# Gate product on VectorE, spectral weights in natural column order, half products, an adding step that sets even and odd columns apart, and a new instruction order

## Chip, cores, metric

One NeuronCore of a Trainium2 chip runs the whole kernel in one launch. The metric is the device time in microseconds, the median of several runs. The engines are TensorE (PE, with weight loads shown apart as PEld), VectorE (DVE), ScalarE (ACT), GpSimd (POOL) and SyncE (SP, which here only issues transfers); ACT issues a few transfers too.

## The reference

x is 2048 x 512 in bf16. Every row gets a gate g; the output mixes a spectral filter of x with a two-layer network of x.

```python
g = _sigmoid((x * gate_w).sum(-1, keepdims=True))
a = irfft2(rfft2(x) * (w_r + 1j * w_i))          # over rows and columns, w is 2048 x 257
b = (mish(x @ w1 + b1)) @ w2                     # w1 512 x 1792, w2 1792 x 512
return g * a + (1 - g) * b
```

## The kernel before, in words

Everything is written as small named tasks (`G.add`), each with its engine, what it reads and what it writes. The string `ORDER` lists all tasks by name; `_Graph.place` walks it and appends each task to the list of its engine, so the order on each of the five engines is fixed by hand. A name may carry an engine (`:dve`) and the slots of its buffers (`::3` is PSUM bank 3, for b2 buffers two banks from there on; DVE scratch `tmp` has three slots). `_Graph.emit` writes the lists out with semaphore waits for the dependencies and for the last users of a slot. Engines run their lists in order, so a task that waits holds up everything behind it on its engine. SP's list holds most transfers, in order too.

The tasks by stage (t is one of 16 row tiles, q one of 4 frequency groups, h a half of its columns):

- `x0`, `x2`, `x4`, `x8`, `x12` (L529) load x into rA (the number is the first tile); `xt8` to `xt15` (L545) load transposed tiles; `tr0` to `tr7` (L567) transpose the other eight on PE, `evx` moves them to xT in rX.
- `bf` (L580): sum and difference of the two halves of x's columns, on DVE or POOL. `p` (L593): a 128-point transform over rows on PE, `ep` its evacuation from PSUM. `d` (L608): the transform over columns, `ed` its evacuation. `t0` to `t3` (L706): 64 small matmuls each that join the 16 row tiles; `et` evacuates to Y in rC.
- W: the spectral weights come in ten pieces (L544) to rS, and 16 copies `wrm...`, `wim...` (L640 and L641, the second kind reading backwards) put them into rW and rA; `wrn` (L655, a transfer) and `win` (L651, DVE) make the second half of the partitions; `wrc`, `wic`, `wrz`, `wiz` patch one column. In rW and rA a row has 132 columns, the even ones first and the odd ones behind them.
- Filter, for each q and h: two copies `sw` (L724) swap the real and imaginary halves of the partitions of Y into `tmp`, `p1` (L733) multiplies Y by rW, `p2` (L736) multiplies `tmp` by rA, `ad` (L739) adds. `c0`, `e1`, `es`, `xp`, `ead`, `e2`, `e3` treat the edge column (`e3`, L781, writes it back).
- `it` (L794), `eit`, `id` (L834), `ec` (L842) and `ey` (L845): the inverse transforms, down to yb in rA. They begin when the filter of their columns is done and need `inv`, `rft`, `zr`, constants and gate values that are loaded late.
- The network: `m{c}_{f}` (L860) is one block of the first layer, four matmuls of 512 columns, for row chunk c (four tiles) and one of 14 blocks f of w1; `h{c}_{f}` (L865) is mish on ACT. 56 such groups. `n{t}` (L878) is the second layer for one tile, 14 matmuls; `ip` (L886, L904) adds the spectral part on PE, `o` and `fin` (L892, L895, L908) scale by the gate, `out` stores. Chunk 3's h is stored in rS, over the staged W, so the first `h3` waits for all W copies.
- The gate: `gate0` and `gate8` (L676), 32 matmuls of one column each with xT; then in two halves a clamp `zcl` (L685), a power on POOL `ez` (L687), `ezb` (L688), `ez1` (L689), `omg` (L690), `gc`. `zt` (L809) transposes it on PE, `zte` (L811) and `zw` send it to DRAM, from where `zr` spreads it.

The first matmuls of the order before, with x0 first, and the place of the last W copies:

```python
x0 tab warm::0 ones ident x2 x4 bf0_1:dve tr0::1 bf2_0:pool tr2::2 evx2:dve cRF x8 graw tr3::3 braw w1_0 evx0:act bf4_0:pool evx3:act bf2_1:dve tr1::4
...
m2_1::3 wim110:dve wic0:pool wrn1 wim101:dve h3_2 ezb8 zt::4 win1 et20:act zte h1_8 sw00_0:dve ez18 sw01_0:dve h3_1 wrz0:dve m0_11::2 h0_11 t3::64
```

Of the kernel before, what the change touches and what calls it, by code (L numbers as in the profile page):

```python
# [333 lines left out]
x0 tab warm::0 ones ident x2 x4 bf0_1:dve tr0::1 bf2_0:pool tr2::2 evx2:dve cRF x8 graw tr3::3 braw w1_0 evx0:act bf4_0:pool evx3:act bf2_1:dve tr1::4  # L334
p2::6 p3 tr7::5 evx1:act w1_4 x12 tr5::0 bf12_0:pool bf4_1:dve bf0_0:dve ep2:act p0::1 p1 ep0:act evx7:dve tr_b::3 evx5:act xt10 tr4::4 tr6::5 p6::6
p7 evx6:act w1_8 bf8_1:dve bf8_0:dve p10::1 p11 xt9 ev_b xt8 m0_0::3 h0_0 cFD wi0s1:sp evx4:dve p4::4 m0_3::0 h0_3 wr0s2:act xt15 ep6:dve ep10:dve
m0_7::6 p5 ep4:act gate0::7 m0_6::3 m1_7::1 wr0s0:sp h0_7 bf12_1:dve h1_7 ebase zcl0 ez0 p8::4 m0_1::2 h0_1 wr0s1:act wr1s0:act wrm001:pool p9 p12::6
p13 ep8:dve p14::0 wr1s1:act ldM0 p15 ep14:dve m1_6::2 m1_2::4 m0_9::5 ezb0 wrm101:pool ep12:act d2::0 d3 ed2:dve d4::6 h0_6 h1_6 h1_2 xt14 d12::2 d5
d13 ed12:dve h0_9 m1_0::4 h1_0 d0::0 d1 ed4:dve wrm011:dve m0_13::5 d8::2 wrm110:pool d9 ed0:act m0_4::4 ed8:act h0_4 wi0s2:act m0_2::0 xt11 h0_2
wi0s0:act wim011:pool h0_13 wim000:pool d6::6 m1_5::1 d7 ed6:dve m0_10::2 d10::3 m0_12::0 xt13 h1_5 m0_5::5 h0_5 xt12 wrm111:pool ldM1 d14::6 h0_12  # L340
d15 ed14:dve m1_9::1 h1_9 h0_10 m0_8::5 h0_8 wi1s1:act m1_3::0 h1_3 wi1s0:sp wim111:pool wim100:pool d11 ed10:act wrm010:dve t0::61 et00:act ez10
wrm000:dve m1_13::5 m1_12::0 h1_12 m2_13::3 h2_13 et01:dve c00 m2_8::4 gate8::1 wim010:dve zcl8 ez8 h1_13 wim001:dve ldM2 win0 wrn0 sw01_1:dve:0
wrc0:pool ldM3 t1::62 et11:act et10:act m1_1::0 h1_1 h2_8 m2_11::5 sw00_1:dve:1 h2_11 m3_1::1 m3_2::2 wrm100:dve t2::63 et21:act c01 m3_5::0 m1_8::5
m2_1::3 wim110:dve wic0:pool wrn1 wim101:dve h3_2 ezb8 zt::4 win1 et20:act zte h1_8 sw00_0:dve ez18 sw01_0:dve h3_1 wrz0:dve m0_11::2 h0_11 t3::64
et31:act m2_4::1 m2_9::2 p1_01:dve p1_00:dve sw11_0:dve:2 wiz0:pool p2_00:pool ad_00:pool sw11_1:dve m2_5::4 m3_10::5 p1_11:dve h2_9 h2_5 m3_3::2
m2_2::4 p2_01:dve p2_11:dve wic1:pool ad_01:pool wiz1:pool ad_11:dve et30:dve c03 h2_4 m2_3::1 h2_3 m2_12::6 sw21_1:dve:2 ldG1 h2_12 h2_2 wrc1:pool
h2_1 c02 zw m1_11::7 m3_13::1 sw31_0:dve:1 wrz1:pool sw31_1:act h1_11 sw21_0:dve sw30_1:dve:0 m2_6::6 h2_6 h3_13 p2_21:dve h3_5 p1_21:dve inv
p1_31:dve m3_12::4 sw30_0:dve h3_3 ad_21:dve p2_31:dve w2_8 ad_31:dve sw10_1:act:2 w2_0 m3_6::3 h3_6 m1_10::7 p2_30:dve edge m2_7::6 omg8 ldG3 h2_7
m3_11::1 h3_11 m3_8::0 h3_8 m2_10::2 h2_10 sw10_0:dve m2_0::3 m3_0::6 p2_10:dve m1_4::1 sw20_0:dve:1 sw20_1:dve p1_20:dve p2_20:dve ad_20:dve m3_4::0
m3_7::2 h1_4 h1_10 p1_10:dve ad_10:dve e1::1 h3_10 es0::1 w2_2 n1_0::7 p1_30:dve ad_30:dve es1 xp1::2 xp2 ead::0 e2::5 h3_7 e3_2 e3_3 h3_4 h2_0  # L350
m3_9::1 h3_0 h3_9 e3_1 it2_0::2 it2_1 e3_0 omg0 o1_0:act it3_0::5 h3_12 ldG0 eit2:dve it3_1 eit3:dve n7_0::0 o7_0:act ldG2 it5_0::2 it5_1 eit5:act
it7_0::6 it7_1 eit7:act it1_0::4 it1_1 n15_0::1 it6_0::2 eit1:dve it4_0::6 it0_0::4 it0_1 eit0:act it6_1 eit6:dve it4_1 n6_0::0 eit4:dve id0::4 id1
id8::2 id9 o6_0:dve id14::6 ec0:dve:1 ey0_1 ey0_0 id15 zr ec8:act:2 n3_0::0 ey8_0 ec14:act:0 ey8_1 ey14_1 n14_0::4 ey14_0 rft rfs ip14_0 o3_0:act
ip15_0 o15_0:act n2_0::5 o14_0:dve id10::2 id4::6 id5 id11 out15_0 ec10:dve:1 ey10_0 o2_0:act ec4:dve:2 ey4_1 id2::0 id3 ey4_0 n0_0::4 o0_0:act
ec2:dve:0 ey2_0 ey10_1 n11_0::5 ip11_0 o11_0:dve id12::6 id13 ec12:dve:2 ey12_1 id6::3 id7 ec6:act:1 ey6_1 ey6_0 n10_0::2 ey12_0 n9_0::5 gc0 ip6::3
fin6 n5_0::4 o5_0:act ip5::6 ip10_0 ip7::7 ey2_1 fin5 ip0::3 out14 ip1::0 n13_0::1 ip13_0 fin1 fin7 ip3::4 out7 n4_0::6 o10_0:dve out11 ip2::0 ip4::7
n12_0::2 fin0 out1 fin2 o4_0:act fin4 ip12_0 out5 o12_0:dve n8_0::3 fin3 out3 ip8_0 o8_0:dve o13_0:act ip9_0 n15_256::6 out13 ip15_256 o9_0:act out9
o15_256:act out15_256
# [3 lines left out]
def _build(nc, A_x, A_w_r, A_w_i, B_x, B_w1, B_b1, B_w2, gate_w, out, merge=8, xtp=8, NWARM=13):  # L362
# [10 lines left out]
    with es:  # L373
# [19 lines left out]
        gw_sb = sb("gw_sb", [128, 4], BF)  # L393
        zcl = sb("zcl", [128, NT], F32)
        junk = sb("junk", [128, 1], F32)
        ebase = sb("ebase", [128, NT], F32)
        ez = zcl
# [11 lines left out]
        Yq = rC[:].rearrange("p (a g h n) -> p a h g n", a=4, g=4, h=2)  # L409
        In = rE[:].rearrange("p (g a k) -> p g a k", g=16, a=4)  # L410
        cinv = rE[:, 0:512].rearrange("p (c m) -> p c m", c=4)
        RFs = rE[:, 2048:4096].rearrange("p (t m) -> p t m", t=NT)
# [9 lines left out]
        EDG = rD[:, 7168:8192].rearrange("p (s c m) -> p s c m", s=2, c=4)  # L422
        cst = w2_sb[:, 0, :]
        RF = w2_sb[:, 1, 0:128]
        FD = cst.rearrange("p (c m) -> p c m", c=4)
        brw = w2_sb[0:18, 1, 128:256]
        ezt = w2_sb[0:NT, 1, 256:384]
        RFT = rE[:, 512:640]
# [537 lines left out]
```

## Time and profile before

| what | value |
|---|---|
| median of three runs | 146.49 us (146.43 to 147.15) |
| the profiled execution, as timed | 148.3 us |
| its span in the profile | 146.3 us |
| mean granted clock of TensorE | 0.965 |
| bytes moved | 17.32 MB, 14463 packets |
| DMA busy, 40 slices | 3999999995364018199910000000010000013132 |

The span is one execution from its first to its last instruction. A slice is 3.66 us; each digit is the busy share in tenths. In a group line, the first number behind the bar is the sum of busy time, the next the mean duration of one in ns, and behind the second bar stands the idle time ahead of such instructions. A duration runs from start to end of one instruction; instructions of DVE that follow each other start a little earlier than the one ahead ends, so the time that one costs in a row of equal ones, called the spacing here, is some 0.07 us less.

### The profile page before, as it was taken

The numbers are of one execution on the slowest core, as the hardware profiler recorded it, in microseconds if no ns is written. First come the engines' busy times: TensorE is split into PE (matmuls) and PEld (weight loads), VectorE is DVE, ScalarE is ACT, GpSimd is POOL, SyncE is SP. The second block draws the span as 40 slices with busy tenths as digits, with TensorE's granted clock in tenths as the row PEclk, the third lists the DMA queues.
The fourth block names the chain that finished last, engine by engine and source line by source line (L and its number), as shares of the span: only waits on it lengthen the run. The fifth ranks groups of instructions, "written<-read, shape, count | busy, mean of one in ns | idle before, by whom it ended". The sixth has DMA issues, their size and how long they took to land.

```text
span 146.3 us, 2775 instructions
## 1 busy us (share of the span) xinstructions
PE 129.9 (89%) x1158; PEld 72.2 (49%) x1174; DVE 97.2 (66%) x131; ACT 65.9 (45%) x97; POOL 40.7 (28%) x30
## 2 busy tenths in 40 slices
PE   7539999999999904996999999999999999999992
PEld 4328665655664501542444465955455454444451
DVE  0397625944999999999999945479418590390440
ACT  4435657785959306551898874612230110101111
POOL 1371540563799963398400000000000000000000
PEclk9995999999999995599999999999999999999999
DMA  3999999995364018199910000000010000013132
GB/s 118 288 349 218 291 192 256 182 291 167 76 139 157 0 39 226 50 283 357 402 64 0 4 0 0 0 4 0 0 54 4 0 0 0 4 73 142 72 143 90
DMA packets 14463, 17.32 MB, mean 118 GB/s; under 512 B 5428, under 2 KB 11444, under 8 KB 14260
## 3 DMA queue, kind: packets, MB, share of 16 engines
q1 hardware_dynamic: 12288, 15.60, 37.5%
q10 hardware_dynamic: 2164, 1.56, 5.7%
q8 instruction: 9, 0.15, 0.4%
q14 instruction: 2, 0.02, 0.0%
HBM read 12.92 MB, written 2.10 MB: 103 GB/s over the span
## 4 chain that ended last, share of the span: by engine, by line
PE 74%; DVE 15%; DMA 4%; issue 4%; ACT 1%; SPq 1%; DVEq 0%
PE ps L878 33%; PE ps L860 26%; DMA rA<-in_A_x_dram 4%; PE ps L593 3%; DVE rA L640 3%; PE ps L834 3%; PE ps L794 2%; PE ps L608 2%; DVE rB L580 2%; DVE rA L641 2%; DVE tmp L724 2%; DVE rW L640 2%; DVE rC L498 2%; DVE gcol L689 1%; PE ps L706 1%
## 5 line engine op out<-in xcount | busy, mean ns | idle before, releaser
L860 PE MATMUL ps<-rX,w_sb 128*128 128x512 bf16 x215 | 51.0, 386 | 2.7 <-DVE rC L498 1.3
L860 PEld LDWEIGHTS ps<-rX,w_sb 128*128 128x128 bf16 x224 | 21.2, 100 | 25.5 <-DVE rC L498 1.8
L878 PE MATMUL ps<-w_sb,hs 128*128 128x512 bf16 x108 | 24.8, 379 | 0.4 <-DVE tmp L842 0.2
L892 ACT ACTIVATE rX<-ps,omg 128x512 bf16<-128x512 f32 (+1 forms) x11 | 7.0, 647 | 36.1 <-PE ps L878 26.6
L865 ACT ACTIVATE hs<-ps,b1f 128x512 bf16<-128x512 f32 x28 | 18.1, 686 | 8.1 <-PE ps L860 6.2
L878 PEld LDWEIGHTS ps<-w_sb,hs 128*128 128x128 bf16 x112 | 10.7, 98 | 12.1
L501 ACT ACTIVATE rC<-ps 128x1024 bf16<-128x1024 f32 x10 | 10.5, 1056 | 8.6 <-PE ps L593 3.8
L878 PE MATMUL ps<-w_sb,rS 128*128 128x512 bf16 (+1 forms) x69 | 12.9, 336 | 0.1
L865 ACT ACTIVATE rS<-ps,b1f 128x512 bf16<-128x512 f32 x14 | 9.2, 691 | 7.5 <-DVE rA L640 6.5
L878 PE MATMUL ps<-w_sb,rD 128*128 128x512 bf16 x54 | 12.3, 379 | 0.2 <-issue 0.2
L908 DVE SCALAR_TENSOR_TENSOR rX<-ps,gcol,rX 128x512 bf16<-128x512 f32 x8 | 5.7, 746 | 9.5 <-PE ps L904 7.0
L865 ACT ACTIVATE rD<-ps,b1f 128x512 bf16<-128x512 f32 x14 | 9.2, 689 | 5.6 <-PE ps L860 5.6
L845 DVE TENSOR_TENSOR rA<-tmp,ps 128x512 bf16<-128x512 f32 x16 | 10.1, 683 | 0.2
L580 DVE TENSOR_TENSOR rB<-rA 128x1024 bf16<-128x1024 bf16 (+1 forms) x7 | 6.6, 967 | 5.4 <-DMA rA<-in_A_x_dram 5.4
L895 DVE TENSOR_SCALAR rX<-ps,omg 128x512 bf16<-128x512 f32 x6 | 4.5, 750 | 8.5 <-PE ps L886 7.6
L498 DVE CAST rC<-ps 128x1024 bf16<-128x1024 f32 x6 | 7.1, 1218 | 3.7 <-PE ps L593 3.7
L498 DVE CAST rE<-ps 128x1024 bf16<-128x1024 f32 x5 | 5.9, 1221 | 5.5 <-PE ps L608 5.5
L878 PEld LDWEIGHTS ps<-w_sb,rS 128*128 128x128 bf16 x70 | 6.8, 98 | 5.5
L498 DVE CAST rF<-ps 128x1024 bf16<-128x1024 f32 x5 | 5.9, 1221 | 4.7 <-PE ps L794 4.7
L878 PEld LDWEIGHTS ps<-w_sb,rD 128*128 128x128 bf16 x56 | 5.4, 98 | 6.5
L593 PE MATMUL ps<-w_sb,rB 128*128 128x128 bf16 x64 | 5.8, 249 | 3.1 <-DVE rB L580 2.4
L736 DVE TENSOR_TENSOR tmp<-tmp,rA 128x1024 bf16<-128x1024 bf16 x7 | 8.4, 1216 | 0.1
(84 smaller groups left out, 163.2 us busy)
## 6 DMA issues: line engine op xcount, KB each, us to landing
w_sb<-in_B_w_dram SPq DMA_DIRECT2D x3, 768.0 KB, 8.4
rF<-c_m SPq DMA_DIRECT2D x4, 512.0 KB, 7.3
rB<-c_g SPq DMA_DIRECT2D x4, 512.0 KB, 7.7
out_dram<-rX SPq DMA_DIRECT2D x7, 256.0 KB, 2.1
rA<-in_A_x_dram SPq DMA_DIRECT2D x3, 512.0 KB, 7.5
rW<-rW SPq DMA_DIRECT2D x2, 528.0 KB, 4.3
w_sb<-in_B_w_dram SPq DMA_DIRECT2D x2, 512.0 KB, 9.2
rS<-in_A_w_r_dram ACTq DMA_DIRECT2D x2, 257.0 KB, 7.3
```

The source lines that it names most:

```text
L498: return e.tensor_copy(out=o(), in_=i())
L501: return e.activation(o(), i(), AF.Copy)
L580: return e.tensor_tensor(out=xu[:, a:b_, uv, :], in0=x_sb[:, a:b_, 0:256], in1=x_sb[:, a:b_, 256:512], op=ALU.add if uv == 0 else ALU.subt ...
L593: ins = e.matmul(bank(b, i)[:, 128 * c:128 * (c + 1)], xu[:, t, uv, e_:256:2], RF, start=True, stop=True)
L640: return e.tensor_copy(out=o_, in_=i_)
L736: return e.tensor_tensor(out=z3(z), in0=z3(z), in1=wi3, op=ALU.mult)
L845: return e.tensor_tensor(out=yb[:, t:t + 2, 256 * h:256 * h + 256].rearrange("p t (i e) -> p t i e", e=2), in0=t4(z), in1=o4(bank(b, 1)), ...
L860: ins = e.matmul(bank(b), w1_sb[:, dt_, 128 * ft:128 * (ft + 1)], xT[:, c, dt_, :, :], start=(dt_ == 0), stop=(dt_ == 3))
L865: G.add(f"h{c}_{ft}", [("act", act(512, 1), lambda e, c=c, ft=ft, b=b: e.activation(hs[c][:, ft, :], bank(b), AF.Mish, bias=b1f[:, ft:ft + ...
L878: ins = e.matmul(bank(b)[:, 0:hi - lo], hs[c][:, ft, 128 * tl:128 * (tl + 1)], w2_sb[:, ft, lo:hi], start=(ft == 0), stop=(ft == NFT - 1 a ...
L892: return e.activation(bs[:, t, lo:hi], bank(b)[:, 0:hi - lo], AF.Copy, scale=omg[:, t:t + 1])
L908: return e.scalar_tensor_tensor(out=bs[:, t, :], in0=bank(b), scalar=gcol[:, t:t + 1], in1=bs[:, t, :], op0=ALU.mult, op1=ALU.add)
```

## The change

- The gate's dot product moves from PE to DVE: `gwm` spreads gate_w over the partitions with one matmul, `gwe` puts it into `tmp`, and 16 tasks `gt` multiply a tile of x by it and sum over the row. The gate's small steps are done once for all 16 tiles.
- rW and rA keep W's columns in natural order (130 to a row). The copies read neighbouring columns; 13 are on DVE, 3 on ACT, none on POOL. Both second halves are made by DVE or ACT (`wrn0`), none by a transfer. W comes in eight pieces.
- The two swaps and the product `p2` of a filter step become two half products `hp`, each on 64 partitions, that read one half of the partitions and write the other. All of the filter is on DVE. `ad` writes to rE instead of in place, and sets even and odd columns apart there; the evacuations `ed` and `et` have another column order. The edge's two copies are gone, `xp2` is in two halves, `e3` one copy instead of four.
- Constants move to other places; `rft`, `inv` and `zr` now lie in rC and wait for the whole filter. w1 comes in four pieces, w2's loads no longer wait for the constants.
- `ORDER` is new: x4 is loaded first; five tiles of the second layer (n7, n6, n4, n5, n0) stand ahead of `it` instead of one (n1).

```diff
+XTP = 8
+W1P = ((0, 2), (2, 6), (6, 10), (10, 14))
+XP = ((0, 2), (2, 4), (4, 8), (8, 12), (12, 16))
-WP = 132
+WP = 130
...
+ebase tab warm::0 x4 ones ident tr6::1 x2 bf4_1:dve bf2_1:pool bf2_0:pool x0 tr4::2 bf4_0:dve w1_2 bf0_0:pool tr5::3 tr2::4 x8 x12 w1_6 cRF evx4:dve
+evx6:dve p4::6 p5 xt11 evx5:dve w1_0 graw::0 braw evx2:act tr3::5 evx3:dve tr_b::0 ev_b ep4:act tr7::2 evx7:dve tr1::1 tr0::3 evx0:dve p6::4 p7 gwm::0
+ep6:dve evx1:act p2::6 p3 w1_10 m0_5::2 gwe:act ep2:act xt8 xt9 bf0_1:pool h0_5 ldM3 m0_4::3 h0_4 gt2 gt5 m1_4::1 h1_4 p0::4 p1 ep0:act m0_3::0 h0_3
+bf8_0:dve bf8_1:dve p8::6 p9 ep8:act xt10 ldM2 bf12_1:dve ldM0 p10::2 p11 ep10:act cFD bf12_0:dve gt14 p12::4 p13 ep12:act m0_6::1 p14::6 m1_6::0 h0_6
+p15 wrs3:act gt1 gt7 m0_8::2 ep14:dve h1_6 gt8 h0_8 ldM1 m0_0::3 h0_0 d2::4 d3 d14::6 wrs0:act d6::0 d7 d15 ed2:act gt13 m0_7::2 h0_7 wrs2:sp ed14:dve
+m0_1::3 h0_1 d0::6 gt11 d1 d8::4 ed0:dve wis2:sp gt12 gt9 d9 ed8:dve ed6:act m1_0::2 h1_0 wis0:sp m2_3::3 d12::6 d13 ed12:dve h2_3 d4::0 d5 ed4:act
+m0_11::2 h0_11 xt15 m2_6::3 h2_6 d10::4 d11 ed10:dve t0::06 et01:act gt10 xt12 gt0 m1_9::2 h1_9 m1_2::3 h1_2 t1::46 et11:dve et00:act wrm111:dve
+et10:act m2_0::2 h2_0 m1_3::3 gt3 t2::06 wrm100:act et21:act wrm110:dve m0_10::4 m2_5::5 wis1:sp wis3:act h2_5 et20:dve c02 m0_2::2 c01 h0_2 gt6 h1_3
+t3::06 gt4 m1_13::5 et31:act et30:act h1_13 gt15 m1_11::2 zcl wim011:act wim101:dve wim110:dve wim100:dve h1_11 m0_12::3 h0_12 m2_9::6 m2_8::7 h2_8
+h2_9 ez m1_1::0 h1_1 m1_10::1 wim111:dve wic1:pool win1:dve wrm101:dve wrc1:pool ezb m2_12::5 xt14 m1_5::2 h1_5 wrs1:sp h1_10 wim000:dve wiz1:dve
+hp31_0::1 m1_7::3 wrm011:act zt::7 h2_12 m2_7::6 h1_7 m2_4::0 h2_4 m2_2::2 hp30_1::2 wrm000:dve h2_2 m0_13::1 wrm010:dve xt13 zte m1_8::7 m3_5::5
+wrm001:dve wim010:dve wrc0:dve h0_10 h1_8 m2_1::3 wim001:dve wrn1:dve wic0:pool win0:dve m3_6::0 hp30_0 h2_1 w2_10 m3_7::2 ldG0 m2_10::4 wrz1:pool
+h2_10 w2_0 ldG2 c03 p1_30 w2_5 m1_12::7 m3_11::3 hp31_1 h1_12 ad_30 h3_11 m3_2::4 h3_2 h0_13 hp21_0::0 wiz0:dve hp10_0::2 hp10_1 m3_12::7 h3_12
+m3_9::3 hp21_1 ez1 omg gc h3_5 h3_9 p1_21 ad_21 hp11_1::0 m3_0::4 wrn0:act n7_0::1 h3_0 zw m3_13::7 m2_13::5 wrz0:dve ldG1 h3_7 m3_10::3 h2_13 n6_0::4
+o6_0:act m3_1::2 c00 n4_0::5 h3_10 p1_31 p1_10 ad_10 h3_1 o7_0:act m3_4::4 hp11_0 h3_13 edge e1::3 m0_9::2 hp01_0::2 p1_11 ad_11 h3_6 hp00_0::0 hp00_1
+hp01_1 n5_0::1 h0_9 o5_0:act p1_00 ad_00 o4_0:act m2_11::7 p1_01 ad_01 ad_31 m3_8::0 xp20::0 xp21 h2_11 xp1::2 ead::1 e2::2 h3_4 hp20_1::0 n0_0::3
+ldG3 h3_8 o0_0:act hp20_0 p1_20 ad_20 e3 rft it7_0::4 it7_1 it6_0::0 eit7:dve it6_1 eit6:act m3_3::7 it0_0::2 it5_0::4 inv it5_1 eit5:dve h3_3 h2_7
+it3_0::0 it3_1 eit3:dve it0_1 eit0:dve n14_0::7 zr it2_0::5 it2_1 it4_0::0 it4_1 eit4:act rfs it1_0::3 it1_1 eit1:act eit2:act n3_0::2 id12::0 id13
...
-        G.add("ev_b", [("dve", 0.25, f_evb)], "small", reads=[bb], writes=["b1f", ("gw", 0)])
...
+        G.add("gwm", [("pe", 0.216, lambda e: e.matmul(bank(gb), one[0:1, :], tb(gwb)[0:1, 512:1024], start=True, stop=True))], "small",
+              reads=[gwb], writes=[gb])
+        evac("gwe", lambda: tb(gwb)[:, 0:512], lambda: bank(gb), 512, [gb], [gwb], "small")
+        t_gt = []
+        for t in range(NT):
+            t_gt.append(G.add(f"gt{t}", [("dve", 0.6, lambda e, t=t: e.scalar_tensor_tensor(
+                out=x_sb[:, t, :], in0=x_sb[:, t, :], scalar=1.0, in1=tb(gwb)[:, 0:512], op0=ALU.mult, op1=ALU.mult, accum_out=zcl[:, t:t + 1]))],
+                "gate", reads=[gwb], writes=[("z", t), ("x", t)]))
...
-            dp = t_bf + t_tr if ri else []
-            base = 64 * ri
+            dp = t_bf + t_tr + t_gt if ri else []
...
-                            i_ = sg[:, 16 * h:16 * h + 16, 0:WP] if pt == 0 else sg[:, 16 * h:16 * h + 16, 256:256 - WP:-1]
-                            i_ = i_.rearrange("p f (k u) -> p f u k", u=2)
-                            o_ = dstv[base + 32 * pt:base + 32 * pt + 32, f0 + 16 * h:f0 + 16 * h + 16, :].rearrange("p f (u k) -> p f u k", u=2)
+                            i_ = sg[:, 16 * h:16 * h + 16, 0:129] if pt == 0 else sg[:, 16 * h:16 * h + 16, 256:127:-1]
+                            o_ = dstv[32 * pt:32 * pt + 32, f0 + 16 * h:f0 + 16 * h + 16, 0:129]
...
-                tg = add("gate", "pe", n * 4 * 0.025, f_gate, [("xT", t) for t in range(t0, t1)] + [("gw", 0)], [gb])
...
-                for j in range(2):
-                    lo = 64 * j
-                    i_ = yv[64 - lo:128 - lo]
-                    G.add(f"sw{q}{h}_{j}", [("dve", 0.37, lambda e, z=z, lo=lo, i_=i_: e.tensor_copy(out=zv(z)[lo:lo + 64], in_=i_)),
...
+                def f_h(e, j, y3=y3, z=z, wi3=wi3, z3=z3):
+                    lo, hi = slice(64 * j, 64 * j + 64), slice(64 - 64 * j, 128 - 64 * j)
+                    return e.tensor_tensor(out=z3(z)[lo], in0=y3[hi], in1=wi3[hi], op=ALU.mult)
...
-                def f_p2(e, z=z, wi3=wi3, z3=z3):
-                    return e.tensor_tensor(out=z3(z), in0=z3(z), in1=wi3, op=ALU.mult)
-
-                def f_ad(e, yv=yv, z=z, zv=zv):
-                    return e.tensor_tensor(out=yv, in0=yv, in1=zv(z), op=ALU.add)
...
+                def f_ad(e, yv=yv, z=z, q=q, h=h):
+                    return e.tensor_tensor(out=Yhq[:, q, h], in0=yv.rearrange("p (x k u) -> p x k u", x=8, u=2), in1=tb(z).rearrange("p (x k u) -> p x k u", x=8, u=2), op=ALU.add)
...
-        dma("inv", rE[:, 0:512], d_inv[:, 1:5, :].rearrange("p c m -> p (c m)"), 0.3, writes=["inv"], deps=t_t)
+        dma("inv", rC[:, 0:512], d_inv[:, 1:5, :].rearrange("p c m -> p (c m)"), 0.3, writes=["inv"], deps=t_fil)
```

Yhq is rE seen as (a, h, x, k, u) with u, the even or odd column, 64 elements apart in memory.

More of the change, by code (lines that the diff above doesn't have):

```diff
@@ L333 @@
 ORDER = """
[L334 to L341, printed above, removed]
@@ L346 @@
[L346 to L349, printed above, removed]
@@ new lines, in _build @@
+        add("zcl", "dve", 0.16, lambda e: e.tensor_scalar(out=zcl[:, :], in0=zcl[:, :], scalar1=80.0, scalar2=-80.0, op0=ALU.min, op1=ALU.max),
+            [("z", t) for t in range(NT)], ["zcl"])
+        add("ez", "pool", 0.9, lambda e: e.tensor_tensor(out=ez[:, :], in0=ebase[:, :], in1=zcl[:, :], op=ALU.pow), ["ebase", "zcl"], ["ez"])
+        add("ezb", "dve", 0.13, lambda e: e.tensor_copy(out=ezb[:, :], in_=ez[:, :]), ["ez"], ["ezb"])
+        add("ez1", "dve", 0.13, lambda e: e.tensor_scalar(out=gcol[:, :], in0=ez[:, :], scalar1=1.0, scalar2=None, op0=ALU.add), ["ez"], ["gcol"])
@@ L779, in _build @@
         G.add("e2", [("pe", 0.2, f_e2)], "edge", reads=[ey_, "edge"], writes=[eb2])
-        for q in range(4):
-            G.add(f"e3_{q}", [("dve", 0.12, lambda e, q=q: e.tensor_copy(out=Y[:, 16 * q:16 * q + 16, 0], in_=bank(eb2)[:, 16 * q:16 * q + 16]))],
-                  "edge", reads=[eb2], writes=[("Yh", q, 0), ("Yh", q, 1)])
+        G.add("e3", [("dve", 0.15, lambda e: e.tensor_copy(out=Yh[:, :, 0].rearrange("p (a j g) -> p a j g", a=4, j=4), in_=bank(eb2)[:, 0:64].rearrange("p (a g j) -> p a j g", a=4, g=4)))], "edge",
+              reads=[eb2], writes=[("Yh", q, h) for q in range(4) for h in range(2)])
         t_it = []
```

195 lines of the change are left out of this document (81 added, 114 removed).

## The prediction, as it was made

> **What bounds the kernel now.** I read the page first (shares of busy time, then the 40 slices), then the list of waits, then the timelines of PE, DVE and POOL.
>
> ```profile
> PE 129.9 (89%) x1158; PEld 72.2 (49%) x1174; DVE 97.2 (66%) x131; ACT 65.9 (45%) x97; POOL 40.7 (28%) x30
> ...
> PE   7539999999999904996999999999999999999992
> ...
> DVE  0397625944999999999999945479418590390440
> ...
> POOL 1371540563799963398400000000000000000000
> PEclk9995999999999995599999999999999999999999
> ```
>
> PE is the bound: nearly full from slice 4 on, with one hole in slices 14 and 15 and a thin head. Beside the hole DVE and POOL are full and PE's clock is halved. The PE timeline shows both places:
>
> ```profile
> 10.52 0.86 PE L593 MATMUL ps<-w_sb,rB 128*128 128x128 bf16 x8 [2.36 <-DVE rB L580]
> ...
> 56.52 0.27 PE L809 MATMUL ps<-identt,ezb 128*16 128x128 bf16 x1 [5.08 <-DVE ezb L688]
> 57.03 1.89 PE L860 MATMUL ps<-rX,w_sb 128*128 128x512 bf16 x4 [0.24 <-ACT rS L865]
> 58.85 1.89 PE L706 MATMUL ps<-rE,rF 32*128 32x128 bf16 x64
> ```
>
> The first number of a line is its start, the second its length, the bracket the idle time ahead of it. After the 5.08 us of idle, four L860 matmuls take 1.89 us (1.03 elsewhere) and 64 of L706 1.89 (1.07): the halved clock costs 1.68 us more. Why DVE was late stands in its waits and rows:
>
> ```profile
> ACT rS L865 <- DVE rA L640: 6.5, 1, 6.5
> ...
> PE ps L860 <- DVE rC L498: 1.3, 1, 1.3
> ```
> ```profile
> L736 DVE TENSOR_TENSOR tmp<-tmp,rA 128x1024 bf16<-128x1024 bf16 x7 | 8.4, 1216 | 0.1
> L733 DVE TENSOR_TENSOR rC<-rC,rW 128x1024 bf16<-128x1024 bf16 x8 | 5.3, 688 | 0.1
> L640 DVE COPY rA<-rS 32x2112 bf16<-32x2112 bf16 x2 | 4.0, 1982 | 0.1
> ```
>
> L736 and L733 have one shape, yet L736 averages 1216 ns against 688: two of seven ran beside a POOL instruction and took 5.00 us together. The rS copies of W end last, ACT's h3 stands behind them, and PE runs out of free banks.
>
> **PE's own work.** Spacings: an mm1 group (four 128x512) 0.8625 us, an mm2 tile (14) 3.02, four 128x128 0.223, a t quarter 1.07. Before, from t0 (37.77) to the inverse transform `it` (86.73): 36 groups 31.05, n1 3.02, four t 4.28, gate 0.78, edge 0.3 = 39.4 in 48.96. The 9.5 lost are 5.08 + 0.24 + 0.33 + 1.30 + 0.48 of small issue gaps + 1.68 of clock, and 0.4 unnamed. The change drops both gate blocks (32 matmuls, 0.78 each) and adds one 128x512 (0.22): PE does 1.34 us less.
>
> **Head.** Before, d began at 24.43 with 9 groups done. x0 and x2 (512 KB) had landed at 5.2, 1 MB at 7.5, 3 MB (x12) at 14.2. In the new order that gives x4 5.2, x2 6.3, x0 7.5, w1_2 9.2, x8 10.8, x12 12.5, w1_6 14.2. DVE sums x4 from 5.2 to 6.5 (0.65 each); POOL does four half-size sums at 1.16 from 6.3 to 10.9, with hardly a DVE sum beside them (in before one DVE sum took 2.34 beside POOL's 2.62). PE waits for x4, then runs transposes, p4 to p7, the gate broadcast and p2, p3 until m0_5 at about 9.5. From there to d2: 8 groups 6.9, eight p 1.8, and p0, p1 0.45 = 9.2, so 18.7. PE idles 1.4 at 3.8 and in pieces afterwards, and in before such a head was followed by a slice at half clock: I add 0.8, d2 at 19.5. d takes 3.57 with 6 groups (5.18) between: t0 at 28.25. This has 14 groups done, before had 20 at 37.77; that is 37.77 - 28.25 - 6 x 0.8625 = 4.3 us earlier, gate included. The x transposes of tiles 8 to 11 are needed at 24.5 now (40 before); xt10 is issued at about 14 by the sum of SP's issue rows (0.5 a plain one, 1.6 to 2.7 a transpose) and takes 7.3 (longest 8.8): landed by 23. W comes in eight pieces instead of ten, with the same bytes, issued from 17 to 24 and landing within 10.2 at the longest row: by 34, wanted from 33 (the first piece, landed by 27) to 48. M0 to M3 are issued ahead of it, by 17, and land in 7.3, where t0 wants them at 28.
>
> **Middle, PE.** 41 groups 35.36, four t 4.28, n7, n6, n4, n5, n0 15.1, edge and zt 0.55, issue gaps 0.64 = 55.9: with no wait, `it` would begin at 84.2.
>
> **Middle, DVE.** Until the clamp of the gate (zcl): it follows t2 (34.9) with an evacuation (1.18), two c0 (0.4) and three gt, so 39.5. The 16 gt are new: 128x512, two inputs with a sum out. Nearest row: L908, the same operation from PSUM, 0.745 long and 0.66 apart; ends: 0.42 (L580 at 512 columns) and 0.82 (0.66 plus a 0.16 small instruction for the sum). I take 0.70: 11.2 us, between the evacuations, where DVE sat idle 1.5 to 2.9 us at a time in before. POOL's power over 16 columns took 1.67 for 8: bounds 1.7 to 3.4, under four W copies either way.
>
> After zcl DVE still has:
> - 11 W copies. Before, they read every second element: 1.24 for 2112 columns. Now they read neighbours, like L724 (0.404 for 1024) and L651 (1.255 for 4224), 0.266 ns a column: 0.68 for 2064. Backwards reads are not shown at this rate; the other end is 1.25, for the four of them 2.3 us more. 7.5.
> - three duplications at 1.25: 3.7. The fourth is on ACT (128x1024 costs 1.02 there: 0.15 + 4160 x 0.85 ns = 3.7), while PE runs n7 and needs no mish; DVE's memset wrz0 waits for it, at about 65 by both counts, and up to 1 us of that stays in the range. They replace two DMA duplications that kept SP's queue waiting until 40.65 and 53.38; now only zw, then edge, hold it, and what stands behind (ldG1, ldG3) is needed at 84.
> - 16 half products at 0.62 (spacing of L733): 9.9, in place of 14 swaps and 7 products. Eight p1: 5.0.
> - eight adds. Six cost 0.62 before; now each output element lands 64 elements from the last one. No row shows that store at this length. Low end: one element a cycle as in L845, 0.61 per 512, so 1.15. For hopping reads: L766 takes 391 ns for 128 columns with W read a row apart, L767 291 without: 0.78 ns each, so 1.15 + 0.75 = 1.9 with rounding. High end: L781 stores 16 hopping elements in 219 ns, L554 14 neighbours in 159: 3.75 ns each, so 5.0; but four of L781 stand only 85 ns apart, so most of that is no rate. I take 1.9, the row with most elements: 15.2.
> - small ones, edge included: 3.2. The evacuations that now set even and odd columns apart read PSUM in hops; L845 does that at 0.61 per 512, so nothing for them.
>
> Sum 44.5, plus three waits for POOL's column copies (0.33 long and two handovers, 0.5 each) 1.5: e3, the last write ahead of `it`, ends at 85.5. That is 1.3 later than PE, so DVE is still the last to arrive, by little.
>
> The Trainium skill ("Vector Engine (DVE) Microarchitecture Reference", 5.2 Measured stream behaviour on trn2) speaks against these adds: a stream that hops at every element takes 1.71 to 1.76 ns a column where neighbours take 1.054, and a store that always steps 24 words takes 2.50. By the first an add would be an estimated 1.83 us and the sum as above; by the second 2.64 and the end near 141. L766 against L767 agrees with the first, for reads and 4-byte elements.
>
> **ACT.** It gains three W copies (1.9 each by its 0.85 ns a column) and loses two swaps; mish needs 0.6 per 0.86 us of PE. I allow 0.5 us for bank waits (0.4 unnamed before). h3 first stands in ACT's order behind the 43rd group, PE near 58, and the last W copy ends near 52: the 5.08 us wait goes, and with it 1.68 of clock.
>
> **End.** Before, `it` to the last matmul (143.51) took 56.78 with 14 tiles and two halves. Four fewer tiles (12.08) and one more group (0.86): 45.6. The constants `inv`, `rft` and `zr` now wait for the last filter; `inv` landed in 2.1 us after issue and is wanted some 10 us after `it` begins, so it hides. The tail stays: 146.3 - 143.5 = 2.8.
>
> **Sum.** 85.5 + 0.5 + 45.6 + 2.8 = 134.4 for the span. The profiled execution of before took 148.3 around a span of 146.3, while the median of the runs is 146.49, 0.2 over that span; so 134.6, and with half a microsecond of doubt towards late, **135.0**.
>
> **The rivals.**
> - *The adds cost one element a cycle (1.15).* DVE ends at 79.5, PE alone decides: 84.2 + 0.5 + 48.4 + 0.2 = 133.3. For: L781's spacing. Chance 0.18, from 131.5 to 133.8.
> - *A store hop costs twice the read hop (2.7 an add), or the backward W copies stay at 1.25 with gt at 0.82.* DVE ends at 92 or 90: 141 or 139. For: nothing in before has such stores at this length. Chance 0.19, from 137 to 143.
> - *The order does less than it says: data come late.* The DMA engines are full until 33 us (the page's DMA row) and much is asked for earlier now: an x transpose or W part that lands 4 us late stops PE or ACT in order, and costs 4 us and up to 1.7 of clock: 138 to 141. Chance 0.09.
> - *Slower: the adds cost what L781's length says (5.0).* Place: the eight adds ahead of e3; PE waits at `it`. 8 x 3.1 = 24.8 more: 159. It decides from 3.5 us an add (12.6 us spread over eight). Against: the 85 ns spacing. Chance 0.09.
>
> **Numbers.** My forecast (134 to 137) has 0.42. Faster by over 0.5% is the forecast and the first three rivals, 0.88; between the third and the last lie 0.03 within 0.5% (0.7 us, about what this measurement can tell); slower 0.09. The range 132 to 142 leaves out the last rival, the far edges of the first and second, about 0.2.
>
> **What would show it.** No PE idle over 1 us between t0 and `it`, clock full there; d from about 19.5 and `it` from 85.5, with e3 just ahead; gt near 0.7, W copies near 0.68 in both directions, adds near 1.9, no DVE row doubled by POOL. Wrong if DVE's adds or gt stand far off, if PE waits for a DMA after 10 us, or if ACT's longer copies leave PE without banks.

## The result, and the profile after

The changed kernel takes **189.19 us** (median of 4 runs, 187.29 to 192.48), the kernel before, timed beside it, 146.82 us (146.43 to 147.45): 1.284 times as long, interval 1.272 to 1.295. The forecast was 135.0 with a range of 132 to 142, so the prediction is wrong, and in its sign. Some executions of a kernel come out over 1.5% longer than its fastest, as 192.48 does here, and the ratios leave these out. The profiled execution took 188.9 us around a span of 186.7.

First the slices of the changed kernel's page (one is 4.67 us here; GB/s is what the DMA engines moved):

```profile
PE   6899799000008999999999800000879999999994
...
PEclk9999999755557999999999975555589999999999
DMA  5999991191199950260000000000011000001413
GB/s 145 364 322 238 377 160 29 33 40 46 49 90 199 379 169 0 52 225 9 0 0 0 0 0 0 0 0 0 4 33 58 0 4 0 32 0 56 183 72 115
```

There are two holes in PE, each five slices wide; the granted clock falls to half in them and stays so for a little behind. Outside of them PE is nearly full from slice 2 on. From slice 6 on and through most of the first hole the DMA engines move 29 to 49 GB/s, against 238 and 377 in slices 3 and 4. The digits of the DMA row do not show how many engines are held: the page counts a packet's whole time in the slice in which it starts, so packets that stand for long leave later slices at one tenth. The list of PE's waits names the holes, and PE's timeline shows their places:

```profile
PE ps L752 <- DVE tmp L745: 24.7, 1, 24.7
PE ps L690 <- issue: 22.9, 1, 22.9
```
```profile
31.98 0.74 PE L690 MATMUL ps<-rE,rF 32*128 32x128 bf16 x40
55.60 0.83 PE L690 MATMUL ps<-rE,rF 32*128 32x128 bf16 x24 [22.88 <-issue]
...
131.12 0.22 PE L752 MATMUL ps<-tmp,rS 128*128 128x1 bf16 x2 [24.67 <-DVE tmp L745]
...
131.68 5.61 PE L854 MATMUL ps<-w_sb,hs 128*128 128x512 bf16 x13 [0.22 <-issue]
...
150.84 2.97 PE L854 MATMUL ps<-w_sb,hs 128*128 128x512 bf16 x13 [0.16 <-DVE tmp L818]
```

The first hole cuts t1 in two after 40 of its 64 matmuls. The matmuls on both sides of it read the same tiles, so no data is missing; "issue" says that the profile shows nothing that PE waited for. The second stands at e2, the edge step, which DVE reaches only at the end of the filter. Behind it 13 matmuls of a tile take 5.61 us, where 13 take 2.97 at full clock.

SP's timeline shows what the transfers did meanwhile. Below it, two groups of DVE show the second hole's cause; the last line is the add of the kernel before (in a group, the number behind the comma is the mean ns of one instruction):

```profile
19.92 30.13 SPq L471 DMA_TRANSPOSE rX<-in_A_x_dram  x2
```
```profile
L715 DVE TENSOR_TENSOR rE<-rC,tmp 128x1024 bf16<-128x1024 bf16 x8 | 37.7, 4754 | 0.2
...
L586 DVE SCALAR_TENSOR_TENSOR rA<-rA,tmp 128x512 bf16<-128x512 bf16 x16 | 11.3, 744 | 0.1
```
```profile
L739 DVE TENSOR_TENSOR rC<-rC,tmp 128x1024 bf16<-128x1024 bf16 x6 | 4.2, 692 | 0.2
```

Two transposes of x took 30.13 us to issue; the sum of SP's rows had put 1.6 to 2.7 on one. L715, the adds, take 4.75 us each where the forecast had 1.9 and the kernel before 0.69 (L739).

The trace's packets tell the rest of the first hole. A merged low piece of W (wrs0, wis0) is 32 packets of 16448 bytes. They went about two at a time: 16.8 us for W_r (23.5 to 40.3), and only then 11.9 us for W_i (40.8 to 52.7). In the kernel before, the 16 packets of the first such piece all started within 0.2 us and took about 1 us each. Something else stood still meanwhile: sixteen packets of 256 and 4 bytes on SP's queue, of the transposes of x by size and place, start near 27 and end together at 53.1, after 25.7 to 26.1 us each and right behind the last of W_i. At 53.1 an instruction packet starts too (the page counts nine of 16 KB each); it landed at 54.2, and PE resumed at 55.6.

### The profile page after: what moved, and what is told of

It is laid out like the page before. It is cut to its first block, busy times and chain, and to the rows that moved or that the text cites. A ratio compares the mean times of both kernels' runs of the same rounds, so it can differ in the third digit from the quotient of the medians.

```text
span 186.7 us, 2660 instructions
## 1 busy us (share of the span) xinstructions
PE 129.2 (69%) x1093; PEld 69.0 (37%) x1111; DVE 123.9 (66%) x158; ACT 76.5 (41%) x101; POOL 10.7 (6%) x16
## 4 chain that ended last, share of the span: by engine, by line
PE 43%; DVE 33%; issue 14%; DMA 5%; ACT 3%; POOL 0%; POOLq 0%; DVEq 0%
DVE rE L715 20%; PE ps L854 18%; PE ps L836 14%; DVE tmp L709 5%; DMA rD<-c_front 3%; DVE rC L712 2%; PE ps L690 2%; DMA rA<-in_A_x_dram 2%; PE ps L810 2%; PE ps L612 2%; PE ps L771 1%; PE ps L862 1%; PE ps L880 1%; PE ps L597 1%; DVE rB L575 1%
## 5 line engine op out<-in xcount | busy, mean ns | idle before, releaser
L715 DVE TENSOR_TENSOR rE<-rC,tmp 128x1024 bf16<-128x1024 bf16 x8 | 37.7, 4754 | 0.2
L868 ACT ACTIVATE rX<-ps,omg 128x512 bf16<-128x512 f32 (+1 forms) x12 | 7.8, 669 | 61.5 <-PE ps L854 37.0
L854 PE MATMUL ps<-w_sb,hs 128*128 128x512 bf16 x107 | 27.4, 409 | 0.6 <-issue 0.4
L502 DVE CAST rC<-ps 128x1024 bf16<-128x1024 f32 x4 | 4.9, 1225 | 26.2 <-PE ps L690 25.2
L505 ACT ACTIVATE rC<-ps 128x1024 bf16<-128x1024 f32 x12 | 12.4, 1069 | 23.9 <-PE ps L690 23.6
L690 PE MATMUL ps<-rE,rF 32*128 32x128 bf16 x256 | 4.8, 223 | 22.9 <-issue 22.9
L752 PE MATMUL ps<-tmp,rS 128*128 128x1 bf16 x2 | 0.2, 177 | 24.7 <-DVE tmp L745 24.7
L690 PEld LDWEIGHTS ps<-rE,rF 32*128 32x128 bf16 x256 | 3.9, 96 | 24.4 <-issue 23.0
L854 PE MATMUL ps<-w_sb,rD 128*128 128x512 bf16 x55 | 12.4, 379 | 0.1
L586 DVE SCALAR_TENSOR_TENSOR rA<-rA,tmp 128x512 bf16<-128x512 bf16 x16 | 11.3, 744 | 0.1
L871 DVE TENSOR_SCALAR rX<-ps,omg 128x512 bf16<-128x512 f32 (+1 forms) x5 | 3.5, 696 | 11.8 <-PE ps L862 7.8
L709 DVE TENSOR_TENSOR tmp<-rC,rA 64x1024 bf16<-64x1024 bf16 x16 | 10.7, 685 | 0.4
L821 DVE TENSOR_TENSOR rA<-tmp,ps 128x512 bf16<-128x512 f32 x16 | 10.2, 681 | 1.0 <-PE ps L810 0.8
```

The lines of the kernel that those rows point to most:

```text
L502: return e.tensor_copy(out=o(), in_=i())
L505: return e.activation(o(), i(), AF.Copy)
L586: t_gt.append(G.add(f"gt{t}", [("dve", 0.6, lambda e, t=t: e.scalar_tensor_tensor(out=x_sb[:, t, :], in0=x_sb[:, t, :], scalar=1.0, in1=tb ...
L690: ins = e.matmul(bank(bp[j // 2], j % 2)[:, 128 * g:128 * g + 128], Mm[r, 4 * q + g, a, :], In[r, 4 * q + g, a, :], start=(a == 0), stop=( ...
L709: return e.tensor_tensor(out=z3(z)[lo], in0=y3[hi], in1=wi3[hi], op=ALU.mult)
L715: return e.tensor_tensor(out=Yhq[:, q, h], in0=yv.rearrange("p (x k u) -> p x k u", x=8, u=2), in1=tb(z).rearrange("p (x k u) -> p x k u", ...
```

## The experiments

Theory: **two faults, each by itself**. (1) The merged W pieces go about two packets at a time, and TensorE's code, which comes as instruction packets among the other DMA packets, is held behind them. (2) The adds' store, which sets each 2-byte element down 64 elements from the last one, costs 4.75 us. The rival to (1): the 22.9 us come from something else in the new order (the transposes, the place in the code). The rival to (2): the adds are dear for their hopping as such, whichever side hops.

**e1_split.** The changed kernel, each merged piece in two:

```diff
...
-            dma(f"{nm}s0", sg[0:64:2], lo, 2.0, queue="sp act", writes=[(nm, "s", 0)])
+            for hh in range(2):
+                dma(f"{nm}s0{hh}", sg[32 * hh:32 * hh + 32:2], lo[hh], 1.0, queue="sp act", writes=[(nm, "s", 0, hh)])
...
```

`ORDER` names the two parts, one behind the other, where it named the piece.

> The changed kernel with each of the two merged W pieces (32 rows of 16448 bytes, one transfer) cut into two transfers of 16 rows, as before the change; nothing else. Theory (serial transfer): the 32 packets of a merged piece went one or two at a time instead of 16 at once, and TensorE's own code, fetched by a transfer as well, stood behind them: the 22.9 us hole inside t1 goes, with some 1.5 us of halved clock; span 160 to 164, packets of 16448 bytes 16 at a time, adds still 4.75 us, TensorE still waiting near 25 us at e2. Rival (the transfers as a whole ask for too much too early, whatever their shape): the hole stays above 15 us, span above 178.

Measured: 168.63 us (168.07 to 170.56), ratio 1.148 (1.139 to 1.157), span 166.5, against 186.7. Its PE waits:

```profile
PE ps L753 <- DVE tmp L746: 24.7, 1, 24.7
PE ps L691 <- issue: 3.1, 1, 3.1
```

The first hole shrinks from 22.9 to 3.1, the second stays. The merge is fault (1); the span lies 2.5 us above the 164 that were expected at most, and the hole that was to go keeps 3.1.

**e2_order.** The changed kernel, with the adds walking in the order of their store, so that the reads hop instead:

```diff
-        Yhq = rE[:].rearrange("p (a h x u k) -> p a h x k u", a=4, h=2, x=8, u=2)
+        Yhq = rE[:].rearrange("p (a h x u k) -> p a h x u k", a=4, h=2, x=8, u=2)
...
-  in0=yv.rearrange("p (x k u) -> p x k u", ...), in1=tb(z).rearrange("p (x k u) -> p x k u", ...)
+  in0=yv.rearrange("p (x k u) -> p x u k", ...), in1=tb(z).rearrange("p (x k u) -> p x u k", ...)
```

> The changed kernel with the eight adds running through the same elements in the order of the store: they write neighbours and read both inputs at a step of two elements; same result in the same place, nothing else. Theory (the hopping store costs): an add falls from 4.75 to 1.15 us, the cost of one element a cycle; the 24.7 us wait at e2 and its halved clock go, span 157 to 161, the 22.9 us hole stays. Rival (the four-dimensional pattern or the two different layouts cost, whichever side hops): adds stay above 3.5 us, span above 178.

Measured: 162.24 us (160.87 to 163.17), ratio 1.101 (1.092 to 1.111), span 161.1. The adds' group and PE's waits:

```profile
L715 DVE TENSOR_TENSOR rE<-rC,tmp 128x1024 bf16<-128x1024 bf16 x8 | 9.7, 1224 | 0.2
```
```profile
PE ps L690 <- issue: 24.7, 1, 24.7
...
PE ps L752 <- DVE tmp L745: 0.3, 1, 0.3
```

The same elements are added, in 1.22 us instead of 4.75: only the side that hops has changed, so the rival to (2) falls. The second hole is gone, the first is whole. In this run the instruction packet that ends the hole is on record from its start: 28.2 us (27.3 to 55.5), where the eight others took 0.9 to 1.4. The packets of the transposes stand here as well, from 27.3 to 54.5.

**e3_both.** Both edits together.

> The changed kernel with both edits: W pieces of 16 rows and adds in the order of the store. If these two are all that the prediction missed, TensorE alone decides and the span is 133 to 136, it begins near 85, no wait of TensorE over 1.5 us after the head. If something else of the new order costs as well, 138 to 146. Slower than before only if neither cause holds.

Measured: 141.65 us (140.3 to 142.36), ratio 0.964 (0.958 to 0.970), so **faster than before**. The spans fall by 20.2 (e1), 25.6 (e2) and 48.5 (both): the faults add up to within 2.7 us. What is left among PE's waits:

```profile
PE ps L691 <- issue: 2.7, 1, 2.7
...
PE ps L772 <- DVE rE L759: 0.7, 1, 0.7
```

The 2.7 are in t1 at the same 40th matmul, and the 64 matmuls of t2 behind them take 1.89 us (1.07 at full clock). So something more than the two faults holds PE there, the second of the two cases that were expected. The packets say that it is code again: counting the later runs too, the trace has eleven holes inside t1 or t3, in nine runs, and at each PE resumes 1.3 to 1.6 us after a 16 KB instruction packet has landed.

**m1_forms.** Single instructions of 128x1024 elements, three of each, and W loads one after the other, with nothing of the computation.

> No part of the computation: single instructions by themselves, each three times and each ended before the next. Adds of 128x1024 in bf16: all neighbours (0.69 expected), the change's hopping store (4.75), the same with neighbours stored and a step of two read (1.15), stores at a step of 2 and of 4 elements, stores in runs of 2, 4 and 16 neighbours, a hopping read on both sides and on one (1.9 by the prediction's price), a hopping store of 4-byte elements, then copies with a hopping store from SBUF and from PSUM, a copy from PSUM with a hopping read (1.22), tensor_scalar and ScalarE's copy with the hopping store. Theory: only stores of lone 2-byte elements are dear (over 4 us), runs of 2 (4 bytes) cost under 2; rival: every hop over 64 bytes costs, whatever its width, so runs of 2 still cost over 2.5 and 4-byte elements over 4. Then transfers one at a time: 32 rows in one transfer to every second partition and to neighbouring partitions, 16 rows in one transfer (twice), 32 rows of 257 in 16 partitions forwards and backwards. Serial theory: both 32-row ones take 15 to 25 us, the 16-row ones 2.5 to 4; rival: all of them take 3 to 6 us when nothing else runs.

Measured, in its groups (L53 stores neighbours; L55 is the changed kernel's add; L57 the same elements in the order of the store; L61 stores every fourth element; L63 and L65 hop between runs of two and of four elements):

```profile
L55 DVE TENSOR_TENSOR o<-a,b 128x1024 bf16<-128x1024 bf16 x3 | 14.1, 4707 | 0.1
...
L61 DVE TENSOR_TENSOR o<-a,b 128x1024 bf16<-128x1024 bf16 x3 | 7.3, 2429 | 0.1
...
L57 DVE TENSOR_TENSOR o<-a,b 128x1024 bf16<-128x1024 bf16 x3 | 3.7, 1226 | 0.1
...
L63 DVE TENSOR_TENSOR o<-a,b 128x1024 bf16<-128x1024 bf16 x3 | 3.1, 1032 | 0.1
L65 DVE TENSOR_TENSOR o<-a,b 128x1024 bf16<-128x1024 bf16 x3 | 2.1, 693 | 0.1
...
L53 DVE TENSOR_TENSOR o<-a,b 128x1024 bf16<-128x1024 bf16 x3 | 2.1, 692 | 0.1
```

The hopping store of lone 2-byte elements costs 4.6 ns an element, runs of two 1.0, runs of four as little as neighbours (0.68). With 4-byte results the same hop takes 1.96 us, on ACT a copy of this form 4.75 (1.06 without hops). The theory holds for this add, but not for every store of lone elements: a step of two costs 1.30 us, a step of four 2.43, a copy from SBUF with the hop of 64 2.49. Hopping reads take 1.23, not the 1.9 of the prediction's price. The merged W load took 18.6 us from its issue to the next, its two 16-row halves 3.7 and 3.5. To neighbouring partitions the merged load took 12.2, below the 15 to 25 that were expected.

**e4_before_merged.** One part of the change alone, in the kernel before: the two low pieces of each W become one.

```diff
...
+ dma(f"{nm}0s0", stg[64 * ri:64 * ri + 64:2], wv[:, 0:64, :].rearrange("q (h l) k -> h q (l k)", h=2), ...)
...
```

> The kernel before with one part alone of the change: the two low W pieces of each array, 16 rows each, become one transfer of 32 rows (W_r on SP's queue, W_i on ACT's), everything else as before. Theory (a 32-row piece of this form is served by one or two DMA engines at a time, about 16 us for its 0.5 MB, and what lies behind it waits, TensorE's code among it): W's copies on POOL and DVE are late or TensorE has a hole with 'issue' before it; 155 to 170 us. Rival (the pieces only hurt in the changed kernel's order, between its transposes of x): within 3 us of the time before.

Measured: 178.93 us (177.71 to 179.65), ratio 1.212 (1.204 to 1.220): the theory's sign, at more than its price. From the waits of all engines:

```profile
POOL rW L644 <- DMA rS<-in_A_w_r_dram: 41.6, 1, 41.6
...
DVE rW L645 <- issue: 33.1, 1, 33.1
...
PE ps L612 <- DVE rE L498: 29.8, 1, 29.8
```

Here it is the data itself that is late. POOL's copy of W waits 41.6 us for the load; DVE stands 33.1 at its own copy from the same staging area (the view names no releaser; that it waits for the load too is argued from its place), with the evacuations of d queued behind, and PE has no bank for 29.8. So this part of the change costs 31 us in the old order too, there by the data and in the changed kernel by the code.

**e5_one_merged.** As e3, but W_r's piece still merged.

> The changed kernel with the adds in store order and W_i's low piece in two transfers, but W_r's low piece still one transfer of 32 rows (on ACT's queue). Theory that each merged piece costs by itself: a hole of 8 us or more inside t1, 147 to 158 us. Rival, that the hole comes from the two in a row (42 to 54 us for the second, behind the first): the hole stays below 4 us and the time is 141 to 144.

Measured: 153.45 us (151.37 to 153.67), ratio 1.035 (1.025 to 1.046).

```profile
PE ps L693 <- issue: 15.5, 1, 15.5
```

One merged piece is enough, and it need not stand on SP's queue with the transposes: this one is on ACT's. It ends at 41.3, though, and the code lands at 46.9. In between W_i's halves, on SP's queue from 26.2 on, go on until 45.3, and packets of the transposes stand until 45.7. In all three runs with a long hole in t1 (the changed kernel, e2, e5) W's pieces, the transposes and the code come free in this order, within 1.6 us. Whether the code stands behind W itself or behind the transposes that W holds up is not shown: no run has a merged piece in this kernel without transposes in flight.

**e6_xt_late** and **e7_xt_late_wic.** What holds the last 2.7 us? e6 is e3 with `xt15` and `xt12` moved behind t3 in `ORDER`; e7 also has `wic1:dve` for `wic1:pool`.

> The kernel with both mended (adds in store order, low W pieces in two transfers), and two of the DMA transposes of x (tokens blocks 15 and 12) issued behind t3 rather than ahead of t0 and t2. Theory (the 2.7 us left inside t1 are TensorE's code held behind traffic that these transposes stretch): the hole falls below 1 us, the granted clock behind it stays above 0.9, 'it' starts 2 to 4 us earlier: 137.5 to 140 us. Rival (the fetch is late at that place of the code whatever the queues hold): the hole stays at 2 to 3 us, 141 to 142.5.

> The last one, and the one-column copy of W_i's second half on VectorE rather than GpSimd, where it waits 3.35 us behind the power of the gate. If VectorE's chain of products sets the start of 'it' once the hole is gone: 1 to 3 us below the last one, 136.5 to 139. If TensorE's own work sets it: the same as the last one within 0.5 us.

Measured: e6 140.74 us, ratio 0.953 (0.946 to 0.960), hole 2.5; e7 139.5 us, 0.944 (0.937 to 0.951), hole 2.6. The transposes were not what holds these last 2.7: the hole kept its size, as e6's rival said. Both times fall between the ranges that were expected for them, and the two intervals overlap, so the 1 us that DVE's wait behind POOL seems to be worth is not settled.

**e8_no_w.** e7 without W's loads.

> The last kernel (both mended, two transposes late, the one-column copy on VectorE) with no spectral weights loaded: their staging area is set to 0.5 by two memsets at the start, so the output is of other weights; all copies and products stay. It takes 2 MB out of the transfers between 18 and 35 us. Theory (the 2.6 us left inside t1 are TensorE's code, asked for near t0's start and held by the traffic): the hole falls below 0.8 us. Rival (two groups of short matmuls one behind the other use up the code faster than it is fetched, whatever the queues hold): the hole stays at 2 to 3 us. The time is then 2 to 3 us lower or the same as the last one within 0.7.

Measured: 135.23 us (135.16 to 135.33), ratio 0.915 (0.910 to 0.920), 4.3 below e7 where 2 to 3 were expected. No hole is left inside a group of matmuls. The windows of e7 and then of e8 (PE, PEld, DVE, ACT and POOL busy, granted clock, DMA share, GB/s):

```profile
30.00:32.00 2.00, 1.84 (x32) 0.86 (x20) 1.81 (x5) 1.61 (x2) 0.00 (x0) 1.00 0.70 140
32.00:34.00 2.00, 0.84 (x41) 0.61 (x41) 0.00 (x0) 1.63 (x3) 0.00 (x0) 1.00 0.99 129
```
```profile
30.00:32.00 2.00, 1.84 (x31) 0.83 (x20) 1.78 (x5) 1.64 (x2) 0.00 (x0) 1.00 1.07 389
32.00:34.00 2.00, 1.84 (x69) 1.36 (x70) 0.81 (x1) 1.83 (x3) 0.00 (x0) 1.00 1.01 349
```

From 30 to 32 us about sixteen packets are in flight in both (the window's share counts a packet where it starts); with W's pieces they move 129 to 140 GB/s in these windows, without them 349 to 389. The instruction packet lands at 34.0 in e7 and at 30.7 in e8, 2 us before PE comes to that matmul. So the last hole too is TensorE's code behind W's traffic, and e6's rival falls: it had looked right only because moving the transposes did not thin out W. W's loads cost e7 some 4 us in all.

**e9_wi_late** and **e10_w_early.** Two other places for W in e7: three W_i pieces behind ACT's evacuations of t0, or four pieces ahead of M's loads.

> The last kernel with nothing left out, and three pieces of W_i issued on ACT's queue behind its evictions of t0 rather than on SP's at 18 to 21 us. If traffic holds the code: less of it at 28 to 33 us, the hole below 1.5 us, 136.5 to 139 us, unless W_i's copies become late (then VectorE waits at the first of them and the time rises to 140 or more). If not: the hole stays at 2.6 us and the time within 0.7 us of the last one.

> The kernel with both mended, two transposes late and the one-column copy on VectorE, and four W pieces (three of W_i, one of W_r) issued ahead of M's pieces on SP's queue instead of behind them, nothing left out. Theory: W's traffic is over sooner and M's pieces, which move more bytes in a unit of time, stand in its place when TensorE's code is asked for; the hole in t1 falls below 1.5 us and no other comes: 136.5 to 139 us. Against it: M then lands too late for t0 (a wait on rF ahead of t0), or the transposes of x ahead of chunk 2 are late: 139.5 to 143.

Measured: e9 141.19 us, ratio 0.953 (0.946 to 0.959), above the 136.5 to 139 that were expected, with a hole of 1.22 in t1 and another of 2.84 in t3: the hole followed the traffic.

```profile
43.34 1.44 PE L691 MATMUL ps<-rE,rF 32*128 32x128 bf16 x45 [2.84 <-issue]
```

e10 took **138.14 us**, ratio 0.931 (0.927 to 0.936), the best of all that compute everything. The ratio rests on three executions of 137.97 to 138.14; two others, one of them the profiled one, took 141.21 and 141.31.

**e11_cfd_early.** e10 with d's constants issued 5 us earlier.

> The last kernel with the constants of d (128 KB) issued some 5 us earlier on ACT's queue, nothing left out. In the last one d waited 2.8 us for them (1.2 in the kernel before that). If that wait is on the path: d begins by 19.5, t0 by 29, and the time falls by 1.5 to 3 us, 135 to 137. If something else holds d (the last p tile, its eviction): less than 0.7 us. The first kernel with both mended twice shows d ahead of time, so the first is the theory.

Measured: 140.96 us, ratio 0.954 (0.946 to 0.962): a miss. Its four executions (140.1 to 141.75) lie at the two upper values of e10, so it gains nothing; that it costs something is not shown. d does begin at 19.77, but what PE gained it gave back further on:

```profile
PE ps L691 <- issue: 2.9, 1, 2.9
...
PE ps L691 <- DMA rF<-c_m: 1.0, 1, 1.0
```

Here the 2.9 stand ahead of the first matmul of t1, not at its 40th, and no code is missing: the instruction packet had landed at 32.6, before PE came there. t1 needs the last piece of M, which was issued at 20.6 and took 15.8 us to land (36.46), and PE resumes at 36.55. So an earlier PE meets two pieces of M that are still being loaded, and the 64 matmuls of t1 take 1.90 us behind the wait, at half clock. "issue" by itself is thus no sign of code.

**m2_outer.** Why is a merged piece served so narrowly?

> Transfers alone, nothing of the computation: six loads from SP's queue, each waited for before the next. The first five move 0.5 MB each: (a) 32 rows of 16448 B read as 2 runs of 16 places, as the changed kernel reads a W piece; (b) 64 rows of 8224 B read as 4 runs of 16 places; (c) 128 rows of 4112 B, 8 runs of 16; (d) 128 rows of 4112 B one behind the other; (e) 32 rows of 16448 B one behind the other; (f) the 16 rows of one split piece, 0.26 MB. Theory (a transfer is spread over as many DMA engines as the outermost loop of its source has steps, up to 16): (a) 10 to 19 us, (b) 5 to 9, (c) 3.5 to 6, (d), (e) and (f) below 4.5. Rival (32 long rows are slow by themselves, whatever their order): (e) takes 10 us or more as (a) does, and (b) is no slower than (d).

Measured in SP's timeline (L67 is (a), L71 is (e); a load lasts from its line's start to the next line's):

```profile
0.73 0.81 SPq L67 DMA_DIRECT2D w<-in_A_w_r_dram  x1
13.29 0.58 SPq L68 DMA_DIRECT2D w<-in_A_w_r_dram  x1
24.48 0.61 SPq L69 DMA_DIRECT2D w<-in_A_w_r_dram  x1
31.36 0.36 SPq L70 DMA_DIRECT2D w<-in_A_w_r_dram  x1
34.77 0.34 SPq L71 DMA_DIRECT2D w<-in_A_w_r_dram  x1
39.26 0.31 SPq L72 DMA_DIRECT2D w<-in_A_w_r_dram  x1
```

(a) 12.6, (b) 11.2, (c) 6.9, (d) 3.4, (e) 4.5, (f) 4.3 us, one execution each; (b) and (c) lie above their ranges of 5 to 9 and 3.5 to 6. (a) and (e) have the same number of packets of the same size into the same number of partitions; the outermost loop of the source, 2 steps against 32, differs (and with it the place of the rows in W). In (f) the rows lie apart as in (a), and all 16 packets are in flight at once. So the rival falls: it is the loop, not the rows. Packets in flight grow with it (2.0, 3.6 and 7.0 on average for 2, 4 and 8 steps, 12.4 in (e)). The Trainium skill states this ("DMA: Bandwidth & Descriptors", Rules for kernel authors): "an outermost dim of size c < 16" confines the whole transfer to at most c engines. These runs agree, by packets in flight; the trace does not name the engine of a packet. The diff had it in plain sight, `"q (h l) k -> h q (l k)"` with h=2.

## Why the prediction was wrong

**The step that failed outright: W "in eight pieces instead of ten, with the same bytes, ... landing within 10.2 at the longest row: by 34".** The longest row was that of a 16-row piece. The merged form stood in no row of before and was given no bounds of its own. Its two transfers took 16.8 and 11.9 us one behind the other; by its packets W_i's ended at 52.7, not by 34. That is 22.9 us in t1 (e1: back to 3.1), and the cost did not come by the way that the rival "data come late" had: nothing waited for W there. The code of TensorE waited, which no step looked at; by which way W holds it, directly or through the transposes, stays open.

**The adds: a term of the sum mis-sized.** The prediction took 1.9 between ends of 1.15 and 5.0; they cost 4.75. Its working chose the read hop of L766 and put down L781's 3.75 ns per element as "no rate", for four of L781 that stood 85 ns apart. That was the wrong row to lean on: L781 is a hopping store of lone 2-byte elements, L766 a read. Nor did the 85 ns speak against a rate: 16 elements at the 4.6 ns of m1 take 74. (The operand of L766 that hops is W, of 2-byte elements, not of 4-byte ones as the working says.) The rival at 5.0, "159" and chance 0.09, had the mechanism and nearly the price: 8 x 2.85 = 22.8 us against 24.7 of wait at e2. The rule of the Trainium skill that it weighed ("Vector Engine (DVE) Microarchitecture Reference", 5.2) goes by 4-byte words; neither of its figures, 1.83 or 2.64 us as estimates, holds for lone 2-byte stores (4.71 in m1). What the page says of adjacent pairs of words does show: runs of four 2-byte elements take 0.69 us, as neighbours do.

**The two terms add**, since t1 and e2 lie one behind the other on PE: 22.9 + 24.7 + 1.3 at `it` are 48.9 of the 52.3 us between the sum of 134.4 and the span of 186.7. The rest is about t0's later start (0.9) and the half clock, 2.6 of it behind the second hole (5.61 against 2.97). The slower side had 0.09 in all, and a rival only for one of the two.

**The rest of the sum held.** x4 landed at 5.3 (5.2). d began at 20.30 (19.5), 1.05 of that a wait for d's constants; t0 at 29.15 (28.25). The 16 gt took 11.3 us (11.2). W copies took 0.70 in both directions (0.68). No PE waits for mish or for zt where 5.08 stood. From `it` at 138.59 to the last matmul at 184.1: 45.5 (45.6), and 2.6 behind it (2.8).

**One cover was missing.** POOL's power over 16 columns took 3.37, the upper bound, "under four W copies either way". They lasted 2.9, and POOL began only behind the third of them. In e3 DVE then stood 3.35 us for POOL's column copy behind the power. The allowance for such waits was 1.5; it was 4.1. e3's adds at 1.22, 5.4 us below the term, paid for that and for some 3 us by which DVE's other instructions exceeded their terms. `it` came at 90.1 instead of 85.5 because the clamp `zcl` ended at 43.6 instead of 39.5, behind t1's hole and its clock. With W's traffic gone and e7's two moves (e8) the span is 133.3. That is the sum of the first rival, whose adds at 1.15 and whose PE that alone decides e8 nearly has; it does not bear out the forecast's 134.4 with adds at 1.9.

## What to carry to other kernels

When transfers are merged, look at the outermost loop of the new pattern before counting bytes: with two steps there, two packets were in flight where sixteen could be, and transposes and code waited behind. When a store would set 2-byte elements apart, see whether it can walk in the order of the store and let the reads hop. Between two candidate rows for an unseen form, take the one with the same side and element size, and if both ends lie far apart give the dear one its share of the chance.

## What the runs showed of the hardware that was not expected

- A matmul stream can stop for want of code with no sign but "issue" in its wait: 22.9 us, after 40 of 64 equal matmuls. What tells it from a wait for data is the instruction packet: it landed 1.3 to 1.6 us before PE resumed at eleven holes, while in e11 it had landed 4.0 before. One such packet took 28.2 us (e2) where others take about 1.
- Behind two merged pieces, sixteen packets of 256 and 4 bytes stood for 25.7 to 26.1 us and ended within 0.1 us of each other.
- Sixteen or more packets in flight can move little: from 30 to 34 us 129 to 140 GB/s with W's pieces among them (e7, in two parts), and 349 to 389 without (e8).
- In an add, a lone 2-byte element stored 64 elements on costs 4.6 ns, four elements on 2.4, two on 1.3; read from there it costs 1.2 ns in all, and in 4-byte form the store costs 1.9. A DVE copy from SBUF with that store costs 2.4 ns an element, one from PSUM 4.6, and one on ACT 4.6.
